# A second sorting pass in chunks of 12 tiles instead of 11, with a run-time check of the row count

## The chip, the cores and the metric

The kernel runs on one core of a Trainium2 chip. A core has a matrix engine (TensorE, PE), a vector engine (VectorE, DVE), an activation engine (ScalarE, ACT), a general engine (GpSimd, POOL) and a sync engine (SyncE, SP). Each takes its instructions from a queue of its own, in order, and they meet through semaphores. The metric is the device time of one execution in microseconds (us); lower is better.

## The reference

The reference is a message-passing layer on a graph with N = 10,000 nodes and E = 640,000 edges. Each node has 64 channels of 4 components. For each edge the source node's features are gathered, multiplied with a small tensor product of the edge's direction, scaled per channel, and summed into the destination node. At the end the channels are mixed.

```python
R = _silu(edge_feat @ w_rad)                        # (E, C), C = 64
xs = x[src]                                         # (E, C, M), M = 4
tp = jnp.einsum('eci,ef,ifo->eco', xs, Y, cg)       # (E, C, M)
msg = R[:, :, None] * tp
agg = _segment_sum(msg.reshape(-1, C * M), dst, N).reshape(N, C, M)
return jnp.einsum('ncm,cd->ndm', agg, w_mix)
```

`src` and `dst` are drawn at random, so the edges come in no order. An edge's own data are 9 words: one word that packs `src` and `dst`, four of `Y` and four of `edge_feat`.

## The kernel before

**The plan.** Edges are handled in tiles of 128, one edge per partition: 5000 tiles. The kernel sorts the edges by destination in two passes on the chip and then works through them bucket by bucket. The first pass sorts into 18 groups of 576 nodes each, the second sorts a group into 18 buckets of 32 nodes. The edges are taken in three parts of 1488, 1776 and 1736 tiles (`SPLIT`). Part 0's first pass runs alone at the beginning. After that three things run side by side, interleaved: the first pass of the next part, the second pass of the next group, and the messages of the current group.

**A pass** (`Pass`, `tables`, `route`) works in chunks of `T` tiles. In both passes a tile's edges are moved by a product with a one-hot matrix, so that the edges of one bucket come together in rows of `r` edges (`r` = 14 in the first pass, 15 in the second). A chunk ends as one array of 128 rows, which one indirect transfer of POOL stores to the rows' places in memory (`store`, line 615; `grp` is the memory of the first pass and `bkt` that of the second). The second pass has `carry`: a bucket's row that is not full at the end of a chunk is not stored but taken over into the next chunk by one more product (line 606). The first pass has T = 12, the second T = 11. The assertion in `Pass` keeps the number of rows of a chunk to 128 at most, in the worst case of all destinations.

**Per chunk**, `route` issues these steps: DVE builds a mask of slots (line 571) and spreads the edges' 9 words over the `r` slots (`X`, line 574). Then the one-hot matrices `oh` are made: `act` of a chunk's tiles on ACT, as a square per tile into `sq` (line 596) and one Relu over all of them (line 597), the others in one comparison on DVE (line 590). `act` is 6 in the first part's first pass and 7 afterwards. With a carried row one more square belongs to ACT. PE multiplies tile by tile into one bank of PSUM (lines 604 and 606), ACT evicts it into `rt` (line 611), and POOL stores it some chunks later. Every two chunks there are also products for the places (534, 536), an eviction (544) and a reduction on DVE (553), and every four chunks three small DVE instructions (559 to 563). `tables` runs once per group in the second pass: it counts the edges of each bucket in each chunk and turns the counts into row numbers; `inc[:N, B - 1:]` in it is the number of rows of each chunk.

**Messages** (`messages`) work in units of 5 tiles (part 0) or 6 (parts 1 and 2): 313 units of part 0, 626 each of parts 1 and 2. Per unit POOL gathers the source features tile by tile (line 911, into `xg`, seven buffers, issued five units ahead), ACT and PE make the radial factor (`pre`, lines 934 to 945), DVE multiplies (line 963) and builds the one-hot factor `S` (953, 956), and PE sums into `G` (line 976). DVE or ACT takes `G` out, from part 1 on with the sum of the part before, fetched from memory through the SP queue (`old`, line 990; `sums`, line 1009). In the last part the mixing product (line 1024) and the output follow.

**What sets the order.** For PE, DVE and ACT the order after the first stage is written out by hand: `groups` walks through the messages' steps and takes from the second pass so many steps per message step that a group is sorted when its messages are due (`pass2_steps`, which counts four steps per chunk). The first stage, with part 0's first pass, has its hand-written order for SP alone; there a planner orders the other engines. POOL's order after the first stage is the planner's too. A sorted group is loaded on the SP queue (line 818) when all its stores have landed; fetches of `old` and stores of `sums` are on the same queue.

**The end.** Rows that found no place in their bucket are kept in an overflow area. `overflow` runs once per pass at the end: it turns the count into a number of loop turns, loads that into registers, and handles 128 edges per turn (`body`).

Of the kernel before, what the change touches and what calls it, by code (L numbers as in the profile page):

```python
# [33 lines left out]
BT = 17  # L34
# [6 lines left out]
FAR = 2097152.0  # L41
# [4 lines left out]
class Pass:  # L46


    def __init__(self, T, r, cap, act, carry):
        self.T, self.r, self.cap, self.act, self.carry = T, r, cap, act, carry  # L50
        self.stride = 1 << (cap + P - 1).bit_length()
        self.rw = r * W

        assert T * P + B * (2 * r - 2 if carry else r - 1) < (P + 1) * r and cap >= P


def weave(main, side, ratio):
# [16 lines left out]
class Kernel:  # L74
    def __init__(self, ctx, tc, x, src, dst, Y, ef, w_rad, cg, w_mix, out):
# [16 lines left out]
        N, E, T, r = self.N, self.E, 12, 14  # L92
# [13 lines left out]
                            for m in e])  # L106
        NG = self.NG
        self.p1 = Pass(T, r, max(map(max, self.gt)) * P // r, 6, False)
        self.p2 = Pass(11, 15, BT * P // 15, 6, True)

        self.gbase = [[(k * NG + g) * self.p1.stride + self.p1.cap - self.gt[k][g] * P // r for g in range(NG)]
                      for k in range(len(SPLIT))]
# [10 lines left out]
            q.rows = q.none  # L123
        self.p1.key, self.p2.key = "grp", "bkt"
        self.xw = max(q.T * q.rw for q in (self.p1, self.p2))
        assert max(q.T + q.carry for q in (self.p1, self.p2)) <= 12

        self.p1.NC, self.p2.NC = 24, max(-(-t // self.p2.T) for t in sum(self.gt, []))
        self.p1.dst = self.dr.tile([self.p1.rows, self.p1.rw], F, name="grp")
# [14 lines left out]
    def consts(self):  # L144
        nc, c = self.nc, self.cst
# [24 lines left out]
        d = iota("dif", [[1, P]], cm=-1, at=self.ph)  # L170
# [47 lines left out]
        self.bn = iota("bn", [[NB, B]])  # L218
        self.bc = c.tile([P, B], F, name="bc")
        nc.vector.memset(self.bc, float(self.p2.cap))  # L220

    def clear_groups(self, k, eng):

# [127 lines left out]
    def tables(self, ps, D, nt, rows, kov, base, cap):  # L351
# [4 lines left out]
        nc, wk, T, r, J, H = self.nc, self.ph, ps.T, ps.r, B + 1, 64  # L356
        N = (nt + T - 1) // T
# [19 lines left out]
        n = w("n", B)  # L377
        nc.vector.tensor_copy(n[:H], sums[:, :, T])
        R = w("R", B)
# [17 lines left out]
        if ps.carry:  # L397

            f, part = w("f", B), w("part", B)
# [11 lines left out]
        inc, st = w("inc", B), w("st", J)  # L411
        nc.vector.tensor_tensor_scan(inc[:H], self.ones[:H, :B], R[:H], 0.0, op0=OP.mult, op1=OP.add)
        nc.vector.tensor_tensor(st[:H, :B], inc[:H], R[:H], op=OP.subtract)
        nc.vector.tensor_copy(st[:N, B:], inc[:N, B - 1:])

        first = w("first", B)
        at = wk.tile([P, XW], F, name="at", tag="x1" + ps.key, bufs=1)[:, :T * B]
# [40 lines left out]
        if ps.carry:  # L458
# [7 lines left out]
                                           op0=OP.is_equal, op1=OP.mult)  # L466
# [7 lines left out]
                                       op0=OP.is_le, op1=OP.mult)  # L474
# [5 lines left out]
        di = w("di", NC, d=I32)  # L480
# [33 lines left out]
    def route(self, ps, quad, nt, table):  # L514
# [5 lines left out]
        N = (nt + T - 1) // T  # L520
# [59 lines left out]
        def rows(c):  # L580

            row, _ = MS[c // (2 * Q)]
            o = c % (2 * Q) * T
            m = min(T, nt - c * T)
            (_, _, _, tg), i = table(c)
            on = ps.carry and i > 0
            oh = self.ph.tile([P, 12, P], F, name="oh", bufs=3)
            v = max(m - ps.act, 0)
            if v:
                nc.vector.tensor_tensor(oh[:, :v, :], self.v128.unsqueeze(1).to_broadcast([P, v, P]),  # L590
                                        row[:, o:o + v].unsqueeze(2).to_broadcast([P, v, P]), op=OP.is_equal)

            at = [row[:, o + u:o + u + 1] for u in range(v, m)] + ([tg[:, i - 1:i]] if on else [])
            sq = self.ph.tile([P, ps.act + 1, P], F, name="sq")
            for u, to in enumerate(at):
                nc.scalar.activation(sq[:, u, :], self.i128, AF.Square, bias=to, scale=-1.0)  # L596
            nc.scalar.activation(oh[:, v:v + len(at), :], sq[:, :len(at), :], AF.Relu, bias=self.ones[:, 0:1], scale=-2.0)  # L597
            XO[c] = (XO[c], oh, m, on)
# [538 lines left out]
    def overflow(self, ps, count):  # L1137
# [12 lines left out]
        n = nc.values_load(ni, min_val=0, max_val=(ps.rows - ps.ovf) * ps.r // P)  # L1150
        flat = ps.dst.rearrange("r w -> (r w)")

        def body(k):
            pay = wk.tile([P, W], F, name="opay")
            nc.sync.dma_start(pay, flat[bass.ds(k * (P * W) + ps.ovf * ps.rw, P * W)].rearrange("(s w) -> s w", w=W))  # L1155
            si = wk.tile([P, 1], I32, name="osi")
            nc.vector.tensor_scalar(si, pay[:, 0:1].bitcast(I32), (1 << 14) - 1, None, op0=OP.bitwise_and)  # L1157
# [5 lines left out]
            xg = wk.tile([P, 64, 4], F, name="oxg")  # L1163
            nc.gpsimd.indirect_dma_start(  # L1164
                out=xg.rearrange("p c i -> p (c i)"), out_offset=None, in_=self.x,
                in_offset=bass.IndirectOffsetOnAxis(ap=si, axis=0))

            pd = pm_.tile([P, 512], F, name="opd", tag="misc", bufs=1)
            nc.tensor.matmul(pd[:, :P], dst.to_broadcast([P, P]), self.ident, start=True, stop=True)
            eq = wk.tile([P, P], F, name="oeq")  # L1170
            nc.vector.tensor_scalar(eq, pd[:, :P], dst, None, op0=OP.is_equal)

            dup = wk.tile([P, P], F, name="odup")
            nc.vector.tensor_tensor(dup, eq, self.L, op=OP.mult)
            skip = wk.tile([P, 1], F, name="oskip")
            nc.vector.tensor_reduce(skip, dup, axis=AX.X, op=OP.max)
            em = wk.tile([P, 1], F, name="oem")
            nc.vector.tensor_scalar(em, dst, 0.5, None, op0=OP.is_lt)
            nc.vector.tensor_tensor(skip, skip, em, op=OP.max)
            di = wk.tile([P, 1], I32, name="odi")  # L1180
            nc.vector.scalar_tensor_tensor(skip, skip, FAR, dst, op0=OP.mult, op1=OP.add)
            nc.vector.tensor_scalar(di, skip, -1.0, None, op0=OP.add)
            cur = wk.tile([P, 256], F, name="ocur")
            nc.vector.memset(cur, 0.0)
            nc.gpsimd.indirect_dma_start(
                out=cur, out_offset=None, in_=self.out, in_offset=bass.IndirectOffsetOnAxis(ap=di, axis=0),
                bounds_check=self.N - 1, oob_is_err=False)

            pT = pm_.tile([P, 512], F, name="opT", tag="misc", bufs=1)
            nc.tensor.transpose(pT[:W, :P], pay, self.ident)  # L1190
            sT = wk.tile([W, P], F, name="osT")
            nc.scalar.activation(sT, pT[:W, :P], AF.Copy)
            pr = pm_.tile([P, 512], F, name="opr", tag="misc", bufs=1)
            nc.tensor.matmul(pr[:, :80], sT, self.wo, start=True, stop=True)
            R = wk.tile([P, 64], F, name="oR")
            nc.scalar.activation(R, pr[:, :64], AF.Silu)
            A = wk.tile([P, 16], F, name="oA")
            nc.scalar.activation(A, pr[:, 64:80], AF.Copy)
            V = wk.tile([P, 64, 4], F, name="oV")
            nc.vector.tensor_tensor(V, xg, R.unsqueeze(2).to_broadcast([P, 64, 4]), op=OP.mult)  # L1200
            M = wk.tile([P, 64, 4], F, name="oM")
            for o in range(4):
                nc.vector.tensor_scalar(M[:, :, o], V[:, :, 0], A[:, o:o + 1], None, op0=OP.mult)
                for i in range(1, 4):
                    nc.vector.scalar_tensor_tensor(M[:, :, o], V[:, :, i], A[:, 4 * i + o:4 * i + o + 1],
                                                   M[:, :, o], op0=OP.mult, op1=OP.add)
            pm = pm_.tile([P, 2, P], F, name="opm", tag="misc", bufs=1)
            for h in range(2):
                nc.tensor.matmul(pm[:, h, :], M[:, 32 * h:32 * h + 32, :].rearrange("p c o -> p (c o)"), eq,
                                 start=True, stop=True)  # L1210
            ms = wk.tile([P, 2, P], F, name="oms")
            nc.scalar.activation(ms, pm, AF.Copy)
            po = pm_.tile([P, 512], F, name="opo", tag="misc", bufs=1)
            for h in range(2):
                nc.tensor.matmul(po[:, :256], ms[:, h, :], self.wx[:, h].rearrange("p d o -> p (d o)"),
                                 start=(h == 0), stop=(h == 1))
            nc.vector.tensor_tensor(cur, cur, po[:, :256], op=OP.add)
            nc.gpsimd.indirect_dma_start(  # L1218
                out=self.out, out_offset=bass.IndirectOffsetOnAxis(ap=di, axis=0), in_=cur, in_offset=None,
                bounds_check=self.N - 1, oob_is_err=False)  # L1220

        with tc.For_i(0, n, 1) as k:  # L1222
            body(k)

    def run(self):
        tile_pool, nc = self.tc.tile_pool, self.nc
# [63 lines left out]
```

## Time and profile before

| | us |
|---|---|
| median of 3 runs | 8613.98 |
| lowest and highest run | 8609.68, 8615.34 |
| the profiled execution | 8636.13 |
| its span, first to last instruction | 8634.0 |
| PE busy | 6890.9 |
| DVE busy | 6821.4 |
| POOL busy | 6034.7 |
| ACT busy | 4619.2 |

The span is cut by what runs: up to about 640 us part 0's first pass and the first group's second pass; from 633.6 us, the first gather, to 8549.6 us, the last one, messages; from there the last sums and the overflow loops. The last store of the first pass starts at 5558.6 us and the last of the second at 8302.1 us. Messages of part 1 begin their gathers at about 3164 us, those of part 2 at about 5964 us.

How to read the rows that follow: a group's row has its line, engine, operation, the tile that is written and those that are read, shapes and count; then busy time and mean duration of one in ns; then the engine's idle time before these instructions and what ended it. "issue" means that the engine waited for nothing that the profile shows. A wait's row has the engine and line that waited, what ended the wait, the total in us, how often, and the longest. A row of the timeline has start, duration, engine, line and operation, and in brackets the idle time before it.

### The profile page before, as it was taken

How to read it: one execution, taken by the hardware profiler on the slowest of the kernel's cores; microseconds unless marked ns; L12 is line 12 of the kernel's file. 1: busy time of each engine (PE TensorE's matmuls, PEld its weight loads, DVE VectorE, ACT ScalarE, POOL GpSimd, SP SyncE). 2: the span in 40 equal slices, each digit the busy share in tenths (PEclk: the TensorE clock that was granted, in tenths of full speed). 3: DMA queues.
4: the chain of work that ended last, by engine and by line, in shares of the span. 5: the costliest groups of instructions: out<-in, count | busy, mean ns of one | idle time of the engine just before them, and what ended most of it. 6: DMA issues, size and time to landing. Idle time of an engine off the chain costs nothing. (4 is left out here: it accounts for less than half of the span.)

```text
span 8634.0 us, 150016 instructions
## 1 busy us (share of the span) xinstructions
PE 6890.9 (80%) x52148; PEld 6320.9 (73%) x52148; DVE 6821.4 (79%) x13093; ACT 4619.2 (54%) x13164; POOL 6034.7 (70%) x6308
## 2 busy tenths in 40 slices
PE   7977888888888778888788888876888878788875
PEld 5867777777777677777777777766777767777764
DVE  7988888888888788898888988876766767676743
ACT  6867666666666465555555655534443434343421
POOL 1226777767777767777777777777777777777775
PEclk9989999999999889999999999988988989898987
DMA  9313444344434434444444444444444444444442
GB/s 160 109 58 101 121 118 119 108 115 117 122 111 116 122 104 134 134 132 138 133 132 137 133 133 133 130 139 130 128 125 125 126 124 124 122 129 124 125 123 83
DMA packets 696294, 1056.68 MB, mean 122 GB/s; under 512 B 252018, under 2 KB 500226, under 8 KB 695536
## 3 DMA queue, kind: packets, MB, share of 16 engines
q0 software_dynamic: 286560, 746.71, 30.3%
q1 hardware_dynamic: 406384, 292.76, 12.6%
q8 instruction: 412, 6.75, 0.3%
q10 hardware_dynamic: 2592, 7.63, 0.3%
q14 instruction: 346, 2.83, 0.1%
HBM read 856.08 MB, written 207.12 MB: 123 GB/s over the span
## 5 line engine op out<-in xcount | busy, mean ns | idle before, releaser
L911 POOL DMA_INDIRECT xg<-in_x_dram,sidx x5321 | 5062.5, 951 | 1713.8 <-issue 1399.6
L604 PE MATMUL pr<-X,oh 128*128 128x126 f32 (+1 forms) x21112 | 2803.6, 291 | 490.1 <-ACT rt L611 321.7
L604 PEld LDWEIGHTS pr<-X,oh 128*128 128x128 f32 x21112 | 2664.2, 202 | 584.8 <-ACT rt L611 377.8
L976 PE MATMUL G<-S,xg 128*128 128x128 f32 x21284 | 2863.7, 296 | 139.0 <-DVE Gp L1005 98.5
L976 PEld LDWEIGHTS G<-S,xg 128*128 128x128 f32 x21284 | 2715.3, 209 | 178.3 <-DVE Gp L1005 120.0
L963 DVE TENSOR_TENSOR xg<-xg,pre 128x1536 f32<-128x1536 f32 (+1 forms) x939 | 1557.8, 1659 | 888.5 <-DMA xg<-in_x_dram,sidx 648.5
L596 ACT ACTIVATE sq<-i,rowf 128x128 f32<-128x128 f32 x6403 | 1969.4, 393 | 21.7 <-DVE rowf L561 21.2
L574 DVE TENSOR_TENSOR X<-dv,Wt 128x1512 f32<-128x1512 f32 (+4 forms) x958 | 1588.4, 1658 | 221.7 <-PE pr L604 171.1
L945 ACT ACTIVATE pre<-pre 128x384 f32<-128x384 f32 (+1 forms) x939 | 431.6, 460 | 1477.3 <-PE pre L942 1125.0
L597 ACT ACTIVATE oh<-sq,ones 128x1024 f32<-128x1024 f32 (+4 forms) x958 | 1017.6, 1062 | 27.4 <-ACT sq L596 0.3
L956 DVE TENSOR_TENSOR S<-dv,pay 128x768 f32<-128x768 f32 (+1 forms) x939 | 857.4, 913 | 60.4 <-PE G L976 15.6
L615 POOL DMA_INDIRECT grp<-rt,idx x417 | 415.3, 996 | 592.5 <-ACT rt L611 256.1
L615 POOL DMA_INDIRECT bkt<-rt,idx x541 | 542.1, 1002 | 219.8 <-issue 129.2
L590 DVE TENSOR_TENSOR oh<-dv,rowf 128x512 f32<-128x512 f32 (+2 forms) x904 | 684.0, 761 | 0.5
L929 PE MATMUL pre<-identb,e 128*108 128x128 bf16 x1878 | 275.2, 230 | 418.4 <-DVE xg L963 410.9
L929 PEld LDWEIGHTS <-e 128*108 128x108 bf16 x1878 | 218.3, 133 | 496.9 <-issue 411.0
L934 ACT ACTIVATE sT<-pre 108x256 bf16<-108x256 f32 x939 | 352.3, 375 | 429.4 <-PE pre L929 428.2
L1024 PE MATMUL po<-wf,Gs 128*128 128x256 f32 (+2 forms) x1392 | 392.7, 445 | 163.6 <-DVE Gs L1005 163.3
L1024 PEld LDWEIGHTS po<-wf,Gs 128*128 128x128 f32 (+2 forms) x1392 | 284.2, 210 | 254.8 <-DVE Gs L1005 179.4
L611 ACT ACTIVATE rt<-pr 128x135 f32<-128x135 f32 (+1 forms) x958 | 258.6, 273 | 259.5 <-DMA bkt<-rt,idx 188.4
L941 PE MATMUL pre<-wr,sT 108*128 108x192 bf16 x939 | 239.7, 255 | 182.4 <-ACT sT L934 180.6
L544 ACT ACTIVATE pc<-pp 128x432 f32<-128x432 f32 (+3 forms) x506 | 243.3, 481 | 251.0 <-DVE pos L553 149.5
(240 smaller groups left out, 5347.5 us busy)
## 6 DMA issues: line engine op xcount, KB each, us to landing
xg<-in_x_dram,sidx POOLq DMA_INDIRECT x5321
sums<-Gp SPq DMA_DIRECT2D x626, 128.0 KB
old<-sums SPq DMA_DIRECT2D x626, 128.0 KB
bkt<-z SPq DMA_DIRECT2D x24, 994.5 KB
pay<-bkt SPq DMA_DIRECT2D x34, 486.0 KB
ys<-in_Y_dram SPq DMA_DIRECT2D x104, 96.0 KB
es<-in_edge_feat_dram SPq DMA_DIRECT2D x104, 96.0 KB
out_dram<-ot SPq DMA_DIRECT2D x69, 128.0 KB
```

What stands on the lines that cost most here:

```text
L574: nc.vector.tensor_tensor(X[:, :m, :].rearrange("p t (s w) -> p t s w", w=W), msk.unsqueeze(3).to_broadcast([P, m, ps.r, W]), QD[c // Q][1 ...
L590: nc.vector.tensor_tensor(oh[:, :v, :], self.v128.unsqueeze(1).to_broadcast([P, v, P]), row[:, o:o + v].unsqueeze(2).to_broadcast([P, v, P ...
L596: nc.scalar.activation(sq[:, u, :], self.i128, AF.Square, bias=to, scale=-1.0)
L597: nc.scalar.activation(oh[:, v:v + len(at), :], sq[:, :len(at), :], AF.Relu, bias=self.ones[:, 0:1], scale=-2.0)
L604: nc.tensor.matmul(pr[:, :ps.rw], oh[:, u, :], X[:, u, :], start=(u == 0), stop=(not on and u == m - 1))
L615: st = nc.gpsimd.indirect_dma_start(out=ps.dst, out_offset=bass.IndirectOffsetOnAxis(ap=idx[:, i:i + 1], axis=0), in_=RT.pop(c), in_offset ...
L911: nc.gpsimd.indirect_dma_start(out=xg[:, t, :], out_offset=None, in_=self.x, in_offset=bass.IndirectOffsetOnAxis(ap=si[:, u:u + 1], axis=0))
L929: nc.tensor.matmul(pre[:KR, 256 + 128 * h:384 + 128 * h], e[:, 36 * t:36 * t + KR], self.identb, start=True, stop=True)
L956: nc.vector.tensor_tensor(S[:, :ut], self.eq[:, :ut].unsqueeze(3).to_broadcast([P, ut, NB, 4]), pb[:, :, 1:5].unsqueeze(2).to_broadcast([P ...
L963: nc.vector.tensor_tensor(V, V, R.unsqueeze(3).to_broadcast([P, ut, 64, 4]), op=OP.mult)
L976: nc.tensor.matmul(G[:, h].rearrange("p n f -> p (n f)"), V[:, t, 32 * h:32 * h + 32, :].rearrange("p c i -> p (c i)"), S[:, t].rearrange( ...
L1024: nc.tensor.matmul(po[:nn, :256], Gs[:, h, f].rearrange("p b n -> p (b n)")[:, :nn], self.wf[:, h, f, :], start=(h + f == 0), stop=(h + f ...
```

## The change

The second pass takes 12 tiles per chunk instead of 11. Its assertion on the worst case of rows now holds for passes without carry alone. In its place `tables` keeps the largest row count of all chunks of the second pass in `most`, one value per chunk number. A new function `whole` runs behind the two overflow loops: it tests whether any count was over 128, loads the answer into registers, and in that case clears the output and handles all edges again, 128 per turn, in a general loop over 5000 tiles. Its loop body, `add`, is the former body of the overflow loop without the loads, which both loops now have for themselves. The tile of one-hot matrices has room for 13 matrices instead of 12, for 12 tiles and the carried row, and the squares `sq` have one buffer instead of two, in all stages.

```diff
-        assert T * P + B * (2 * r - 2 if carry else r - 1) < (P + 1) * r and cap >= P
+        assert (carry or T * P + B * (r - 1) < (P + 1) * r) and cap >= P
...
-        self.p2 = Pass(11, 15, BT * P // 15, 6, True)
+        self.p2 = Pass(12, 15, BT * P // 15, 6, True)
...
-        assert max(q.T + q.carry for q in (self.p1, self.p2)) <= 12
+        self.ot = max(q.T + q.carry for q in (self.p1, self.p2))
...
+        self.most = c.tile([64, 1], F, name="most")
+        nc.vector.memset(self.most, 0.0)
...
         nc.vector.tensor_copy(st[:N, B:], inc[:N, B - 1:])
+        if ps.carry:
+            nc.vector.tensor_tensor(self.most[:N], self.most[:N], inc[:N, B - 1:], op=OP.max)
...
-            oh = self.ph.tile([P, 12, P], F, name="oh", bufs=3)
+            oh = self.ph.tile([P, self.ot, P], F, name="oh", bufs=3)
...
-            sq = self.ph.tile([P, ps.act + 1, P], F, name="sq")
+            sq = self.ph.tile([P, ps.act + 1, P], F, name="sq", bufs=1)
...
-        def body(k):
+        def load(k):
             pay = wk.tile([P, W], F, name="opay")
...
+            return pay, si, dst
 
         with tc.For_i(0, n, 1) as k:
-            body(k)
+            self.add(*load(k))
+
+    def whole(self):
+
+        nc, wk = self.nc, self.ph
+        m = wk.tile([64, 1], F, name="om")
+        nc.vector.tensor_scalar(m, self.most, P + 0.5, None, op0=OP.is_ge)
+        cp = self.ps.tile([P, 512], F, name="cw", tag="misc", bufs=1)
+        nc.tensor.matmul(cp[0:1, 0:1], self.ones[:64, 0:1], m, start=True, stop=True)
+        ni = wk.tile([1, 1], I32, name="nw")
+        nc.vector.tensor_scalar(ni, cp[0:1, 0:1], 1.0, None, op0=OP.min)
+        n = nc.values_load(ni, min_val=0, max_val=1)
+        assert self.N % 125 == 0
+        zo = wk.tile([125, 256], F, name="zo")
+        nc.vector.memset(zo, 0.0)
+
+        def load(k):
+            pay = wk.tile([P, W], F, name="opay")
+            nc.vector.memset(pay, 0.0)
...
+            return pay, si, dst
+
+        with self.tc.For_i(0, n, 1):
+            nc.sync.dma_start(self.out.rearrange("(p b) f -> p b f", p=125),
+                              zo.unsqueeze(1).to_broadcast([125, self.N // 125, 256]))
+            with self.tc.For_i(0, self.NT, 1) as k:
+                self.add(*load(k))
+
+    def add(self, pay, si, dst):
...
             self.overflow(self.p1, self.kov[:, 0:1])
             self.overflow(self.p2, self.kov[:, 1:2])
+            self.whole()
```

More of the change, by code (lines that the diff above doesn't have):

```diff
@@ L1162, in body @@
             nc.vector.tensor_scalar(dst, dk, 1.0 - TD, None, op0=OP.add)
[L1163 to L1220, printed above, removed]
-        with tc.For_i(0, n, 1) as k:
-            body(k)
+            return pay, si, dst
+        with tc.For_i(0, n, 1) as k:
+            self.add(*load(k))
[14 more added lines that the diff above has]
+            nc.vector.memset(pay, 0.0)
+            si = wk.tile([P, 1], I32, name="osi")
+            dk = wk.tile([P, 1], I32, name="odk")
+            t = bass.ds(k, 1)
+            nc.sync.dma_start(si, self.src[:, t])
+            nc.sync.dma_start(dk, self.dst[:, t])
+            nc.sync.dma_start(pay[:, 1:5], self.Y[:, t, :].rearrange("p t f -> p (t f)"))
+            nc.sync.dma_start(pay[:, 5:9], self.ef[:, t, :].rearrange("p t f -> p (t f)"))
+            dst = wk.tile([P, 1], F, name="odst")
+            nc.vector.tensor_scalar(dst, dk, 1.0, None, op0=OP.add)
+            return pay, si, dst
[4 more added lines that the diff above has]
+                self.add(*load(k))
```

56 lines of the change are left out of this document (added).

## The prediction

> **What bounds the kernel now.** I read the page's shares first, then the busy time by stretch, then who waits for whom, then the order of GpSimd's (POOL's) instructions. By the shares three engines stand close together, so the shares alone name no bound. The five stretches after the first line give, for each, its length, then busy time and instruction count of PE, PE's weight loads, DVE, ACT and POOL, then clock and DMA.
>
> ```profile
> PE 6890.9 (80%) x52148; PEld 6320.9 (73%) x52148; DVE 6821.4 (79%) x13093; ACT 4619.2 (54%) x13164; POOL 6034.7 (70%) x6308
> ...
> 0.00:640.00 640.00, 504.31 (x3753) 441.50 (x3754) 549.50 (x1317) 457.42 (x1377) 137.60 (x155) 0.91 0.50 109
> ...
> 1000.00:3000.00 2000.00, 1646.61 (x12953) 1531.17 (x12953) 1697.84 (x3306) 1278.98 (x3729) 1456.49 (x1514) 0.92 0.41 117
> ...
> 3500.00:5500.00 2000.00, 1648.71 (x12902) 1535.23 (x12902) 1748.54 (x3233) 1166.44 (x3291) 1518.28 (x1582) 0.92 0.46 133
> 5500.00:8550.00 3050.00, 2379.59 (x17090) 2160.35 (x17089) 2065.62 (x3651) 1181.30 (x3232) 2310.56 (x2423) 0.89 0.44 127
> 8550.00:8634.00 84.00, 30.48 (x111) 21.24 (x110) 24.95 (x101) 3.61 (x14) 11.53 (x13) 0.58 0.05 15
> ```
>
> POOL is busy for only 76% of the two long late stretches, yet it issued 1582 transfers in 2000 us and 2423 in 3050 us: one per 1.264 and 1.259 us, the same pace under two different loads of the other engines. The order of POOL's work, around one store to `bkt`, says why.
>
> ```profile
> 7012.34 0.95 POOL L911 DMA_INDIRECT xg<-in_x_dram,sidx  x1 [0.30 <-issue]
> 7013.59 0.95 POOL L911 DMA_INDIRECT xg<-in_x_dram,sidx  x1 [0.30 <-issue]
> 7014.84 1.01 POOL L615 DMA_INDIRECT bkt<-rt,idx  x1 [0.30 <-issue]
> 7016.15 0.96 POOL L911 DMA_INDIRECT xg<-in_x_dram,sidx  x1 [0.30 <-issue]
> ```
>
> A gather takes the queue from 7013.59 to 7014.84, 1.25 us; a store from 7014.84 to 7016.15, 1.31 us. The 0.30 us before each belongs to the pace: nothing is waited for. So POOL is full there although it shows 76%. The waits (total us, times, longest us) confirm it; in order they are POOL's from 3500 to 5500 and from 1000 to 3000, DVE's from 5500 to 8550 and two from 3500 to 5500, and one of the SP queue's over the whole span.
>
> ```profile
> POOL xg L911 <- issue: 343.4, 1127, 0.3
> POOL xg L911 <- DMA grp<-rt,idx: 11.9, 39, 0.3
> ...
> POOL xg L911 <- PE G L976: 48.0, 28, 6.0
> ...
> DVE xg L963 <- DMA xg<-in_x_dram,sidx: 604.2, 154, 6.5
> ...
> DVE Gp L1005 <- DMA sums<-Gp: 44.0, 6, 15.4
> DVE xg L963 <- DMA xg<-in_x_dram,sidx: 7.0, 2, 3.7
> ...
> SPq L818 <- DMA bkt<-rt,idx: 809.6, 45, 34.8
> ```
>
> From 5500 on DVE waits 604.2 us for gathers: POOL sets the time. From 3500 to 5500 POOL's listed waits are all 0.3 us, but DVE hardly waits for gathers (7.0 us), so either could be the slower. The counts up to 3500 and up to 5500 decide: gathers issued, and units (5 gathers for the first 313, then 6) whose product DVE has begun.
>
> ```profile
> L911 POOL DMA_INDIRECT xg<-in_x_dram,sidx x1781: 942/946/1327, 633.6 to 3498.0; - x198
> L963 DVE TENSOR_TENSOR xg<-xg,pre x345: 1468/1478/1756, 716.1 to 3496.9; 128x1280 f32<-128x1280 f32 x157, 128x1536 f32<-128x1536 f32 x16
> ...
> L911 POOL DMA_INDIRECT xg<-in_x_dram,sidx x3113: 942/946/1367, 633.6 to 5497.8; - x195
> L963 DVE TENSOR_TENSOR xg<-xg,pre x567: 1468/1489/1756, 716.1 to 5496.3; 128x1280 f32<-128x1280 f32 x105, 128x1536 f32<-128x1536 f32 x84
> ```
>
> At 3500 the lead is 1781 - (1565 + 32 x 6) = 24 gathers, at 5500 it is 3113 - (1565 + 254 x 6) = 24. Two independent rates would not agree so well over 2000 us. I read it as POOL holding the others back through its stores: the load of a sorted group on the SP queue waits for the group's last store (809.6 us in 45 waits), and the partial sums that queue behind it on SP make DVE wait (44.0 us in 6). That link is inferred. From 1000 to 3000 it is the other way round: POOL waits 48.0 us for buffers that PE frees, and DVE (85%) and PE (82%) with their mutual waits set the pace.
>
> **The change, part by part.** *Chunks.* A group of part 0, 1, 2 has 95, 113, 111 tiles, the small last group 40, 47, 46. By 11 that is 9, 11, 11 chunks (4, 5, 5), by 12 it is 8, 10, 10 (4, 4, 4): 541 chunks become 488. The 53 that go are 17 of part 0 and 18 each of parts 1 and 2. Each takes with it one store on POOL, one carry product on PE, one eviction on ACT and one each of the DVE's per-chunk instructions; the tiles stay the same.
>
> ```profile
> L615 POOL DMA_INDIRECT bkt<-rt,idx x346: 971/1005/1078, 3499.3 to 8302.1; - x173
> ...
> L590 DVE TENSOR_TENSOR oh<-dv,rowf 128x512 f32<-128x512 f32 x487 | 332.2, 682 | 0.4
> L590 DVE TENSOR_TENSOR oh<-dv,rowf 128x640 f32<-128x640 f32 x292 | 238.0, 815 | 0.0
> ...
> L574 DVE TENSOR_TENSOR X<-dv,Wt 128x1485 f32<-128x1485 f32 x487 | 830.7, 1706 | 82.4 <-PE pr L604 53.8 <-DVE dv L571 0.5 <-PE pre L942 0.5
> L574 DVE TENSOR_TENSOR X<-dv,Wt 128x945 f32<-128x945 f32 x18 | 20.6, 1144 | 14.7 <-PE pr L604 13.4
> ...
> L553 DVE TENSOR_REDUCE pos<-pc 128x22 f32<-128x396 f32 x243 | 134.8, 555 | 10.5 <-ACT pc L544 10.5
> ...
> L559 DVE TENSOR_SCALAR row<-pos 128x44 int32<-128x44 f32 x104 | 24.2, 233 | 3.6
> ...
> L596 ACT ACTIVATE sq<-i,rowf 128x128 f32<-128x128 f32 x6403 | 1969.4, 393 | 21.7 <-DVE rowf L561 21.2
> ...
> L606 PE MATMUL pr<-rt,oh 128*128 128x135 f32 x974 | 198.0, 286 | 54.6 <-ACT rt L611 54.6
> ```
>
> POOL after 3500: 346 stores are left, part 2's 192 and 154 of part 1, so groups 4 to 17 of part 1. By 12 they are 18 and 14 fewer: 32 x 1.31 = 41.9 us, all on the path if POOL stays full.
>
> DVE: with 7 of a chunk's tiles on ACT, DVE's share of the one-hots grows from 4 to 5 tiles. A group of part 1 or 2 goes from 10 x 0.682 to 9 x 0.815 = +0.52 us, one of part 0 from 8 x 0.682 to 7 x 0.815 + 0.682 = +0.93. Against it: the two L574 rows differ by 0.562 us over 540 elements, 1.04 ns each, which leaves 0.16 us fixed per instruction; a chunk less saves that in L574, L571 and L553, 0.47 us. Part 0 also drops one of three groups of slots, three instructions of the kind of L559 (0.233): 0.7. The longest count adds one small instruction per group, 0.13 to 0.17 by the rows below. Sum: +0.2 us a group in parts 1 and 2, -0.1 in part 0, some +6 us in 8000, hidden wherever POOL sets the pace and 0.1% where DVE does.
>
> ACT: squares fall from 4095 to 3745 (8 fewer in a group of part 0, 6 in parts 1 and 2): 350 x 0.393 = 138 us. PE: 53 carry products in two instructions each, 53 x 2 x 0.286 = 30 us. Neither engine is full, so this counts only through shorter waits.
>
> Before 3500 these two waits (DVE for PE, PE for ACT, both from 1000 to 3000) tell what a chunk's handing over costs.
>
> ```profile
> DVE X L574 <- PE pr L604: 87.9, 33, 8.5
> ...
> PE pr L604 <- ACT rt L611: 154.5, 78, 5.1
> ```
>
> 21 of the 53 chunks go there, of 195 of the second pass (541 - 346) and, an estimate from the code's counts, 175 of the first (part 1's 148 and the start of part 2's 145): about 6%. 6% of 87.9 to 154.5 us is 5 to 9 us in 2000, 8 to 13 us in the 2860 us from 640 to 3500. I take -8 us. Ends: -27 (21 x 1.31, POOL's whole saving passed on) and +18 (17 x 0.93 + 4 x 0.52, DVE's larger one-hots with none of its savings).
>
> *One buffer of squares, in all stages.* Squares and the Relu that reads them both run on ACT, in order, so a new square after the old Relu is what the queue does anyway.
>
> ```profile
> L597 ACT ACTIVATE oh<-sq,ones 128x1024 f32<-128x1024 f32 (+4 forms) x958 | 1017.6, 1062 | 27.4 <-ACT sq L596 0.3
> ...
> L597 ACT ACTIVATE oh<-sq,ones 128x768 f32<-128x768 f32 x124 | 115.2, 929 | 0.0
> ```
>
> The Relu, which already waits for squares just written, loses 27.4 / 958 = 0.03 us; the mirror wait would cost the same, 124 x 0.03 = 4 us at most in the first stage, off the path of DVE (86% busy there). I take 0, with ends -4 and +4.
>
> *The check behind the loops, and the fallback.* After the last overflow iteration come a comparison, a one-column product, its conversion, the load of the count into registers, and a loop with no turns. The first pass's overflow loop has no turns now; its price stands here, with the small instruction nearest to the longest count's and two turns of the second loop.
>
> ```profile
> 8571.56 0.13 DVE L1149 TENSOR_SCALAR ni<-kov 1x1 int32<-1x1 f32 x1
> 8576.26 0.21 PE L1142 MATMUL cp<-kov,ones 1*16 1x1 f32 x2 [6.89 <-issue]
> ...
> 8580.64 0.15 DVE L1157 TENSOR_SCALAR osi<-opay 128x1 int32<-128x1 int32 x1 [2.98 <-DMA opay<-bkt]
> ...
> 8599.20 0.15 DVE L1157 TENSOR_SCALAR osi<-opay 128x1 int32<-128x1 int32 x1 [1.38 <-DMA opay<-bkt]
> ...
> L414 DVE COPY st<-inc 11x1 f32<-11x1 f32 (+7 forms) x85 | 11.4, 134 | 0.0
> L413 DVE TENSOR_TENSOR st<-inc,R 64x18 f32<-64x18 f32 x85 | 14.5, 170 | 2.7
> ```
>
> From the count's conversion to the first work behind the empty loop are 4.7 us. I take +5 for the new one; ends +2 and +10 (the loop is nested). It can't gain: it stands after the last work. The overflow's own three turns stay, since with carried rows a bucket's row total does not depend on the chunk.
>
> Sum: -41.9 - 8 + 0 + 5 = -45 us. The profiled execution took 8636.13 us with a span of 8634.0; the median of the runs is 8613.98, 22 us less. I take the same difference there: 8569 us, and 8591 for a profiled one.
>
> **Rivals.** *DVE is the bound in part 1 (within 0.2%).* Then part 1's 14 stores are worth nothing, and before 3500 nothing is won: -18 x 1.31 + 5 + 3 (DVE, part 1) = -16 us, 8598. For it: DVE is 87% busy from 3500 to 5500, the fullest engine on the page. Against it: the lead of 24 gathers that does not move. The Trainium skill, Perfetto Trace Analysis, section Identifying the Most-Contended Engine, takes occupancy as the sign of the bottleneck and would choose this rival, DVE's 87% over POOL's 76%; by that rule the time is 8598. The trace speaks against it in POOL's unbroken pace, which occupancy leaves out.
>
> *The single buffer breaks the overlap in the first stage (slower).* There the order on ACT isn't written out by hand, and now a chunk's squares cannot be placed ahead of the Relu before. If each of the 124 chunks then shows its Relu of 0.929 us to DVE and PE: +115, 8684. It turns the sum to slower by over 0.2% from (45 + 17) / 124 = 0.50 us a chunk. Against it: 0.3 us of waits for squares in all, and DVE, not ACT, is full there.
>
> *More is won early (faster still).* ACT and PE, relieved, free the gather buffers sooner and POOL's 48.0 us of waits go: 8521.
>
> *The fallback runs.* If a chunk had over 128 rows, 5000 turns of 18.56 us (8580.64 to 8599.20) would follow, over 90,000 us. A full chunk has 1536 / 15 = 102.4 rows and at most 18 x 28 / 15 = 33.6 more, 136; each bucket's two ends add 14 / 15 of a row on average, 119 in all; the phases of 18 buckets spread that by one or two rows. So it should not run.
>
> **How the numbers follow.** A measurement tells 0.2%, 17 us, from no change. Forecast 0.60, with its own range from 8614 - 42 - 27 + 2 - 4 = 8543 to 8614 - 42 + 18 + 10 + 4 = 8604; DVE as the bound 0.16; single buffer 0.12; more early 0.11; fallback 0.01. So faster 0.71, same 0.16, slower 0.13. The range leaves out the slower cases and most of the largest gain: 8530 to 8622.
>
> **What would show it.** Right: 488 stores to `bkt`; from 3500 to 8550 one POOL transfer per 1.26 us as before, and a group of part 2 shorter by 1.3 us; the first gather at 633.6 as before; some 5 us more behind the last scatter. Wrong: POOL waiting after 3500 (then DVE bounds part 1), the first gather later (the squares), or ACT's waits for `bkt` stores growing at the change of part.

## The result

The changed kernel takes 8537.26 us in the median of 6 runs (8534.49 to 8543.41), the kernel before 8610.93 us in 6 runs beside it: a ratio of 0.9915 with a 95% interval of 0.9905 to 0.9925, 73.7 us less. The prediction had the sign, and the time lies in its range, near the fast end; the gain forecast was 45 us.

In the page of the changed kernel the totals moved as the counts said: DVE 12 us more, ACT 151 us less, POOL 51 us less. The line is the page's first.

```profile
PE 6849.6 (80%) x51885; PEld 6294.3 (74%) x51885; DVE 6833.0 (80%) x12901; ACT 4467.9 (52%) x12655; POOL 5984.1 (70%) x6255
```

The two spans are 8634.0 and 8537.6 us, 96.4 us apart, more than the medians. So the kernel before was profiled a second time (before_again, below); that execution had a span of 8605.1 us. Against it the spans differ by 67.5 us, 6 us less than the medians, and these can be laid out by part. The next rows are the busy time by stretch, first of the second execution of the kernel before, then of the changed kernel; each stretch begins with a part's first gather, the last ends with the last gather. The columns are the stretch, its length, then busy time and count of PE, weight loads, DVE, ACT and POOL, clock and DMA.

```profile
617.70:3136.10 2518.40, 2056.11 (x16232) 1907.81 (x16232) 2154.58 (x4271) 1621.09 (x4724) 1815.30 (x1888) 0.92 0.40 115
3136.10:5935.80 2799.70, 2251.75 (x17580) 2096.89 (x17581) 2378.25 (x4427) 1553.55 (x4370) 2114.36 (x2206) 0.91 0.46 133
5935.80:8520.40 2584.60, 2036.17 (x14488) 1844.36 (x14488) 1716.69 (x2999) 980.98 (x2683) 1958.85 (x2053) 0.89 0.43 125
```

```profile
614.00:3108.60 2494.60, 2041.02 (x16132) 1902.07 (x16133) 2152.49 (x4162) 1553.28 (x4508) 1796.88 (x1870) 0.92 0.40 116
3108.60:5885.40 2776.80, 2231.63 (x17475) 2079.01 (x17474) 2383.82 (x4384) 1511.64 (x4222) 2096.86 (x2186) 0.91 0.46 134
5885.40:8448.30 2562.90, 2045.20 (x14416) 1854.95 (x14415) 1726.99 (x2953) 936.54 (x2542) 1942.34 (x2037) 0.87 0.43 126
```

| | before, second execution | after | difference |
|---|---|---|---|
| to the first gather | 617.7 | 614.0 | -3.7 |
| part 0's gathers | 2518.4 | 2494.6 | -23.8 |
| part 1's gathers | 2799.7 | 2776.8 | -22.9 |
| part 2's gathers | 2584.6 | 2562.9 | -21.7 |
| from the last gather's start to the end | 84.7 | 89.3 | +4.6 |

How far such lengths can be trusted is shown by two kernels below that differ little from these: the same parts take 2519.3, 2803.7 and 2585.7 us in sq1_only, 2497.0, 2778.6 and 2564.5 us in no_check. So a difference of up to 4 us in a part means nothing here, and the 3.7 us before the first gather are no part of the gain: the first gather is at 609.4 us in sq1_only and at 609.8 in no_check.

In part 2 POOL issued 2053 transfers before, one per 1.259 us, and 2037 after, one per 1.258: the pace is the same and the number fell. In part 1 it is 1.269 and 1.270 us. Of the 17, 18 and 18 chunks that the parts save, the rows show 18, 20 and 16, because a part's second pass begins before its messages do, and a transfer across the border of two stretches counts in both. DVE's waits from 3500 to 5500 us in the kernel before (total, times, longest), and then POOL's and DVE's in the changed kernel:

```profile
DVE X L574 <- PE pr L604: 45.7, 21, 7.5
DVE Gp L1005 <- DMA sums<-Gp: 44.0, 6, 15.4
...
DVE Gp L1005 <- issue: 31.3, 4, 15.8
```

```profile
POOL xg L915 <- issue: 345.2, 1133, 0.3
...
DVE Gp L1009 <- DMA sums<-Gp: 67.6, 8, 24.2
DVE Gp L1009 <- issue: 60.9, 6, 15.6
...
DVE X L578 <- PE pr L608: 22.9, 15, 5.8
```

POOL's 0.3 us steps are there as before. DVE's waits for PE fell from 45.7 to 22.9 us, and its waits around the partial sums, which come over the SP queue, grew from 44.0 + 31.3 to 67.6 + 60.9. That fits a DVE that isn't the bound here: relieved in one place, it waits in another.

Of the prediction's signs of being wrong none came: POOL's listed waits from 3500 us to the last gather are of 0.3 us but for one of 5.2, the first gather is not later, and ACT's longest wait for stores to `bkt`, at the change to part 2, is 36.8 us after 42.2 in before_again.

### The profile page after: what moved, and what is told of

It is laid out like the page before. It is cut to its first block, busy times and chain, and to the rows that moved or that the text cites. A ratio compares the mean times of both kernels' runs of the same rounds, so it can differ in the third digit from the quotient of the medians.

```text
span 8537.6 us, 148817 instructions
## 1 busy us (share of the span) xinstructions
PE 6849.6 (80%) x51885; PEld 6294.3 (74%) x51885; DVE 6833.0 (80%) x12901; ACT 4467.9 (52%) x12655; POOL 5984.1 (70%) x6255
## 5 line engine op out<-in xcount | busy, mean ns | idle before, releaser
L608 PE MATMUL pr<-X,oh 128*128 128x135 f32 (+1 forms) x21112 | 2783.1, 291 | 400.2 <-ACT rt L615 256.8
L600 ACT ACTIVATE sq<-i,rowf 128x128 f32<-128x128 f32 x6106 | 1876.1, 392 | 5.6 <-DVE rowf L565 2.4
L578 DVE TENSOR_TENSOR X<-dv,Wt 128x1512 f32<-128x1512 f32 (+3 forms) x905 | 1579.7, 1746 | 147.0 <-PE pr L608 100.0
L601 ACT ACTIVATE oh<-sq,ones 128x896 f32<-128x896 f32 (+2 forms) x905 | 964.3, 1066 | 28.8 <-issue 1.4
L594 DVE TENSOR_TENSOR oh<-dv,rowf 128x640 f32<-128x640 f32 (+2 forms) x870 | 719.3, 831 | 0.5
L619 POOL DMA_INDIRECT bkt<-rt,idx x488 | 488.6, 1001 | 192.5 <-issue 111.2
L896 ACT ACTIVATE e<-er 128x360 bf16<-128x360 f32 (+3 forms) x420 | 188.9, 450 | 416.1 <-DVE er L906 415.5
L548 ACT ACTIVATE pc<-pp 128x432 f32<-128x432 f32 (+4 forms) x453 | 233.5, 515 | 254.2 <-DVE pos L557 131.9
```

What stands on the lines that cost most here:

```text
L578: nc.vector.tensor_tensor(X[:, :m, :].rearrange("p t (s w) -> p t s w", w=W), msk.unsqueeze(3).to_broadcast([P, m, ps.r, W]), QD[c // Q][1 ...
L608: nc.tensor.matmul(pr[:, :ps.rw], oh[:, u, :], X[:, u, :], start=(u == 0), stop=(not on and u == m - 1))
L619: st = nc.gpsimd.indirect_dma_start(out=ps.dst, out_offset=bass.IndirectOffsetOnAxis(ap=idx[:, i:i + 1], axis=0), in_=RT.pop(c), in_offset ...
```

## The experiments

Beside the first four experiments the kernel before took 8610 us; beside change_again, extra_squares_2, act8_2 and split_108, on another chip, 8620.6 us. Four runs (extra_squares, sq2_first, extra_products, act8) met a third chip, on which the kernel before itself takes 10,497 us; there they can be compared with each other and with the kernel before, but not with the 8537 us.

### before_again: the same kernel, a second profile

No edit.

> The kernel before, unchanged, for a second profiled execution. If the 20 us by which the first gather came earlier (633.6 us before, 614.0 after) belong to the change, the first gather stands again within some 5 us of 633.6 and the last within 15 us of 8549.6. If they belong to that one execution, the first gather comes near 614 and the span near 8611.

Measured: 8607.25 us, span 8605.1, first gather at 617.7, last at 8520.4 us. So 16 of the 20 us before the first gather, and about 12 of the 35 us in part 0, that the first two traces seemed to show belong to that one execution of the kernel before.

### sq1_only: one buffer of squares alone

```diff
-            sq = self.ph.tile([P, ps.act + 1, P], F, name="sq")
+            sq = self.ph.tile([P, ps.act + 1, P], F, name="sq", bufs=1)
```

> The kernel before with one buffer of squares and nothing else. Theory of the prediction (squares and Relu are in order on ACT anyway): 8611, within 5 us, first gather as in the kernel before. Rival (the single buffer changes the order that the planner gives the first stage, and for the better): first gather 15 to 20 us earlier, total 8591 to 8596. Second rival (it costs): up to 8726.

Measured: 8612.4 us in 10 runs, ratio 1.0003 (0.9993 to 1.0012); first gather at 609.4 us. The single buffer neither costs nor brings anything that can be measured here.

### no_check: without the longest count and the check

```diff
-        if ps.carry:
-            nc.vector.tensor_tensor(self.most[:N], self.most[:N], inc[:N, B - 1:], op=OP.max)
...
-            self.whole()
```

> The changed kernel without the longest count and without the check and the general loop behind it (the two other parts of the change stay). The check was priced at 5 us: 8537 - 5 = 8532, and from the last gather to the span's end 84 us instead of 89. If the longest count, one small DVE instruction per group, also costs where DVE is full, up to 9 us more is won: 8523.

Measured: 8536.18 us, ratio to the kernel before 0.9912 (0.9895 to 0.9929), not told apart from the changed kernel. The trace has the price. The rows are the last scatter and the check behind it in the changed kernel (span 8537.6), then the last scatter without the check (span 8538.1).

```profile
8530.33 1.03 POOL L1264 DMA_INDIRECT out_dram<-ocur,odi  x1 [8.68 <-DVE ocur L1263]
8533.72 0.19 PE L1178 MATMUL cw<-om,ones 64*1 64x1 f32 x2 [4.13 <-issue]
8533.94 0.14 DVE L1180 TENSOR_SCALAR nw<-cw 1x1 int32<-1x1 f32 x1 [3.90 <-PE cw L1178]
```

```profile
8533.86 1.03 POOL L1262 DMA_INDIRECT out_dram<-ocur,odi  x1 [8.68 <-DVE ocur L1261]
```

From the last scatter's start to the end it is 7.3 us with the check and 4.2 without: 3 us. The rest of the 4.6 us by which the end grew has another source: the overflow loop's first turn takes 22.9 us in the changed kernel (8477.00 to 8499.85), 23.0 in no_check and 18.6 in the kernel before, while the loop begins 2.7 us sooner after the last gather in the changed kernel. In extra_stores, which has the check as well, the first turn takes 18.7 us again, and in split_108 21.4, so neither the check nor the chunks of 12 alone make it; the cause is open.

### extra_stores: POOL's transfers put back, nothing else

`nowhere` holds an index out of bounds, so these 51 stores write nothing.

```diff
+            at = [idx[:, i:i + 1]] + ([self.nowhere] if ps.carry and N > 4 and c == 4 else [])
+            rt = RT.pop(c)
-            st = nc.gpsimd.indirect_dma_start(
-                out=ps.dst, out_offset=bass.IndirectOffsetOnAxis(ap=idx[:, i:i + 1], axis=0),
-                in_=RT.pop(c), in_offset=None, bounds_check=ps.none - 1, oob_is_err=False)
+            sts = [nc.gpsimd.indirect_dma_start(
+                out=ps.dst, out_offset=bass.IndirectOffsetOnAxis(ap=a, axis=0),
+                in_=rt, in_offset=None, bounds_check=ps.none - 1, oob_is_err=False) for a in at]
```

> The changed kernel with one more transfer on POOL for each of the 51 large groups, a store whose rows all lie outside the bounds, so that nothing is written; POOL's number of transfers is that of the kernel before again, and everything else stays. Theory (POOL's queue is the bound after 3500 us, each store 1.31 us): 31 of them fall after 3500, +41 us, 8578, and with POOL's share before 3500 passed on in part up to +55, 8592. Rival (DVE is the bound in part 1): +22 us from part 2 alone, 8559. If POOL is nowhere the bound: 8537. A store that writes nothing may be shorter than 1.31 us; then the sum goes by its measured pace.

Measured: 8590.06 us in 9 runs, ratio 0.9974 (0.9964 to 0.9984): 53 us of the 73.7 are gone again. The first rows are its three parts, the last ones POOL's order around one of the added stores.

```profile
611.60:3117.00 2505.40, 2045.03 (x16133) 1906.22 (x16134) 2147.84 (x4162) 1551.21 (x4508) 1814.15 (x1889) 0.92 0.40 116
3117.00:5916.00 2799.00, 2243.97 (x17469) 2092.57 (x17468) 2383.75 (x4384) 1510.85 (x4221) 2113.72 (x2204) 0.90 0.46 133
5916.00:8500.10 2584.10, 2062.74 (x14426) 1873.09 (x14426) 1727.91 (x2953) 934.86 (x2542) 1958.65 (x2053) 0.86 0.43 125
```

```profile
7007.96 1.00 POOL L625 DMA_INDIRECT bkt<-rt,idx  x1 [0.30 <-issue]
7009.27 1.00 POOL L625 DMA_INDIRECT bkt<-rt,nowi  x1 [0.30 <-issue]
7010.57 0.98 POOL L922 DMA_INDIRECT xg<-in_x_dram,sidx  x1 [0.30 <-DMA bkt<-rt,idx]
```

An added store takes 1.30 us of the queue (7009.27 to 7010.57) although it moves nothing. The added stores bring part 1 from 2776.8 to 2799.0 and part 2 from 2562.9 to 2584.1 us, 22.2 and 21.2 us: all but 0.7 and 0.5 us of what the change won there. By the rows the two stretches hold 34 transfers more (2186 and 2037 before, 2204 and 2053 now), 1.28 us each. DVE and ACT are as busy there as in the changed kernel, within 2 us, and the counts of PE's instructions agree within 10. So POOL's queue is the bound in both parts, which the rival with DVE as part 1's bound does not survive. In part 0 they bring 10.8 of 23.8 us back.

### change_again: the changed kernel on another chip

> The changed kernel, unchanged, beside the kernel before on the same chip as the next three, so that they have their base. On the chip of the first comparisons: 8537 beside 8610. If the chip is the one of extra_squares, sq2_first, extra_products and act8, on which the kernel before takes 10497 us and POOL's queue is not full: the theory that the gain is POOL's gives no gain there, 10480 to 10520; if the gain came from ACT, PE and fewer chunks handed over, it stays and grows, 10400 to 10440.

Measured: 8550.58 us beside 8620.63, ratio 0.9919 (0.9903 to 0.9936); parts of 2492.5, 2778.2 and 2563.7 us. This is the base of extra_squares_2, act8_2 and split_108.

### extra_squares_2 and act8_2: what ACT's relief was worth in part 0

The first repeats 349 squares, the second gives ACT an eighth tile of each chunk of the second pass.

```diff
+            if ps.carry and c % 4:
+                nc.scalar.activation(sq[:, 0, :], self.i128, AF.Square, bias=at[0], scale=-1.0)
```

```diff
-            self.p1.act = self.p2.act = 7
+            self.p1.act, self.p2.act = 7, 8
```

> The changed kernel with 349 squares done twice on ACT in the second pass, as in extra_squares, now beside the changed kernel. Of part 0's 23 us (2518.5 us from its first gather to part 1's in the second execution of the kernel before, 2495 after), POOL's transfers gave back 10.7 in extra_stores. If the other 12 are ACT's relief: part 0 at about 2507 us, total 8549. If they are not: part 0 within 4 us of 2495, total within 8 us of the changed kernel's. Parts 1 and 2 stay at 2777 and 2563 in both cases.

> The changed kernel with 8 instead of 7 of a chunk's tiles on ACT in the second pass, as in act8, now beside the changed kernel. DVE has some 58 us less to do, ACT some 217 more. If DVE sets part 0's pace: part 0 10 to 20 us shorter, 8517 to 8527. If the way through ACT does: part 0 10 to 40 us longer. Part 2, where POOL is full, stays at 2563 us.

Measured: 8563.32 us (8561.08 to 8565.65) and 8574.7 us (8569.0 to 8577.63), 13 and 24 us above the changed kernel's 8550.58. The rows are part 0 of the changed kernel (change_again), of extra_squares_2 and of act8_2.

```profile
619.10:3111.60 2492.50, 2037.06 (x16106) 1898.75 (x16107) 2146.78 (x4161) 1549.76 (x4503) 1795.87 (x1871) 0.92 0.41 117
```

```profile
620.90:3134.30 2513.40, 2050.45 (x16133) 1911.13 (x16134) 2149.70 (x4162) 1584.01 (x4622) 1798.75 (x1871) 0.92 0.40 116
```

```profile
622.40:3141.90 2519.50, 2065.08 (x16129) 1924.32 (x16130) 2129.80 (x4162) 1610.42 (x4657) 1795.30 (x1870) 0.91 0.40 115
```

In the traces the loss is in part 0: +20.9 and +27.0 us, while parts 1 and 2 stay within 3 us (2775.4 and 2563.3; 2779.7 and 2564.6). These are more than the medians' 13 and 24 us, since the profiled execution of change_again, with 8545.23 us, is the fastest of its four. 119 more ACT instructions with 34 us of work lengthen part 0 by 21 us by the traces, 13 by the medians, though ACT is busy for only 62% of it. In act8_2 DVE has 17 us less to do and part 0 is longer all the same: DVE at 86% does not set part 0's pace alone. The waits that grow are PE's for ACT's evictions; the rows are from part 0 of change_again, then of extra_squares_2, then of act8_2.

```profile
PE pr L608 <- ACT rt L615: 141.6, 67, 5.6
```

```profile
PE pr L610 <- ACT rt L617: 170.4, 74, 5.9
```

```profile
PE pr L608 <- ACT rt L615: 187.8, 81, 6.0
```

In the changed kernel's first trace the same wait is 157.4 us, so 16 of the 29 us by which extra_squares_2 is above change_again are within the spread. One such wait in extra_squares_2 shows the order on ACT: seven squares, the extra one (L602), the Relu, and only then the eviction that PE has waited for.

```profile
1661.27 2.15 ACT L600 ACTIVATE sq<-i,rowf 128x128 f32<-128x128 f32 x7
...
1663.62 0.39 ACT L602 ACTIVATE sq<-i,rowf 128x128 f32<-128x128 f32 x1
1664.03 1.15 ACT L603 ACTIVATE oh<-sq,ones 128x1024 f32<-128x1024 f32 x1
...
1665.62 0.28 ACT L617 ACTIVATE rt<-pr 128x135 f32<-128x135 f32 x1
...
1665.95 2.39 PE L610 MATMUL pr<-X,oh 128*128 128x135 f32 x9 [5.43 <-ACT rt L617]
```

An eviction stands in ACT's queue behind the squares of the next chunk, PE waits for the bank, and DVE waits for PE (60.1, 71.5 and 83.1 us in the same three). POOL in turn waits for what comes late: in part 0 its waits of over 0.4 us sum to 147.7 us in change_again, 169.5 in extra_squares_2 and 179.2 in act8_2, and these sums differ by what the lengths of part 0 differ by, within 5 us.

### The four runs on a chip where PE is slower

extra_squares and act8 have the edits just shown. sq2_first has two buffers of squares in the first stage and one afterwards; extra_products adds one product with zeros on PE for each large group.

```diff
-            sq = self.ph.tile([P, ps.act + 1, P], F, name="sq", bufs=1)
+            sq = self.ph.tile([P, ps.act + 1, P], F, name="sq", bufs=self.sq_bufs)
```

```diff
+            if ps.carry and N > 4 and c == 4:
+                nc.tensor.matmul(pr[:, :ps.rw], oh[:16, 0, :], self.zr[:, :ps.rw], start=False, stop=False)
```

> The changed kernel with 349 squares done twice on ACT in the second pass (in chunks 1, 2, 3, 5, 6, 7 and 9 of a group), 349 x 0.392 = 137 us of ACT, so that ACT has as many squares as in the kernel before. If part 0's gain of 35 us (first gather to part 1's first gather, 2530 us before and 2495 after) came from ACT's relief: +15 to +35 us, all before 3200 us, 8552 to 8572. If it came from POOL or from fewer chunks handed over: 8537, within 8 us. After 5500 us no change in either.

> The changed kernel with two buffers of squares in the first stage again (one afterwards, as in the changed kernel). If the single buffer made the first stage faster: first gather back at about 633 us, 8552 to 8557. If it had no part in it: first gather at 614, 8537, within 5 us.

> The changed kernel with one more product with zeros on PE for each of the 51 large groups (two PE instructions of some 0.29 us), so that PE has the carry products' time of the kernel before again, 51 x 0.58 = 30 us. If PE's relief earned part 0's gain: up to +10 us (17 groups x 0.58), 8547. Otherwise 8537, within 5 us.

> The changed kernel with 8 of a chunk's 12 tiles on ACT in the second pass, 4 on DVE as with 11 tiles. DVE has 434 fewer tiles of one-hots, some 434 x 0.133 = 58 us, ACT 434 more squares with their share of the Relu, some 434 x 0.5 = 217 us. If DVE sets the pace in part 0: some 20 us faster, 8517. If the hand-overs to and from ACT do: 10 to 40 us slower, 8547 to 8577. After 5500 us, where POOL is full, no change.

Measured: 10551.85, 10522.81, 10517.61 and 10576.07 us beside 10496.59 for the kernel before, ratios of 1.0056, 1.0025, 1.0022 (1.0012 to 1.0031) and 1.0069. The rows are one stretch of the changed kernel on the first chip, then two of extra_products and its POOL waits from 1000 to 3000 us.

```profile
1000.00:3000.00 2000.00, 1643.09 (x13032) 1533.74 (x13031) 1731.76 (x3316) 1250.46 (x3635) 1463.60 (x1523) 0.92 0.41 119
```

```profile
0.00:640.00 640.00, 507.86 (x3749) 442.48 (x3749) 546.40 (x1309) 462.35 (x1373) 137.47 (x151) 0.91 0.49 108
...
1000.00:3000.00 2000.00, 1500.04 (x10552) 1364.76 (x10552) 1405.14 (x2694) 1015.13 (x2952) 1161.66 (x1205) 0.84 0.33 94
```

```profile
POOL xg L917 <- issue: 252.8, 827, 0.7
POOL xg L917 <- PE G L982: 173.1, 62, 8.4
```

The first stage is as fast as elsewhere; then PE gets through 10,552 instructions in 2000 us where it did 13,032 in the changed kernel, at a granted clock of 0.84 instead of 0.92, and POOL waits 173.1 us for PE. Why is open. One question of the four is answered: the first gather is at 640.5 us with two buffers of squares in the first stage and at 637.2 (extra_squares), 638.1 (extra_products) and 646.9 us (act8) with one, so no part of the single buffer in the first stage is to be seen. Among themselves, extra_squares is 29 us and act8 53 us slower than sq2_first, as on the other chip in sign, and extra_products is 5 us faster, within the spread of its runs. The price of PE's products alone was not measured on a chip where POOL is full. What the runs suggest besides, and no more, is that the gain is not there when POOL's queue has room: sq2_first, the changed kernel but for the first stage's buffers, is 26 us slower than the kernel before. The changed kernel itself did not run on that chip.

### split_108: a faster version

If POOL's stores are the bound in parts 1 and 2, the next chunk to save is part 2's last one: 111 tiles are 9 chunks and 3 tiles.

```diff
-SPLIT = ((0.3, (5,)), (0.355, (6,)), (0.345, (6,)))
+SPLIT = ((0.3, (5,)), (0.365, (6,)), (0.335, (6,)))
```

> The changed kernel with four chunks of the first pass moved from part 2 to part 1 (1824 and 1688 tiles instead of 1776 and 1736). A large group of part 2 then has 108 tiles, 9 chunks instead of 10, and one of part 1 has 116, still 10. Theory (POOL is the bound in parts 1 and 2): part 2 is 17 x 1.31 = 22 us shorter, part 1 4 x 1.31 = 5 us shorter by the first pass's stores; part 0 is up to 13 us longer, as four more chunks of the first pass run beside it: 8537 - 22 - 5 + 13 = 8523. A turn less or more of the overflow loop behind it would change this by 18 us either way. If the stores of part 2 are worth nothing: 8545.

Measured: 8512.88 us (8510.61 to 8517.01), ratio to the kernel before 0.9876 (0.9859 to 0.9892), 37.7 us less than the changed kernel beside it, where 14 were expected. The rows are its three parts.

```profile
618.00:3107.60 2489.60, 2048.55 (x16181) 1909.47 (x16182) 2161.82 (x4176) 1563.31 (x4534) 1799.51 (x1872) 0.91 0.41 117
3107.60:5874.10 2766.50, 2255.43 (x17518) 2100.83 (x17517) 2377.35 (x4349) 1509.42 (x4209) 2095.03 (x2183) 0.91 0.47 135
5874.10:8418.60 2544.50, 2033.62 (x14257) 1842.90 (x14256) 1709.52 (x2920) 907.62 (x2453) 1928.63 (x2021) 0.89 0.44 127
```

Part 2 is 19.2 us shorter with 16 transfers fewer (2037 to 2021), 1.2 us each, as POOL's pace says. The rest was not foreseen: part 1 is 11.7 us shorter, more than its 3 transfers fewer (2186 to 2183) account for, and part 0 did not grow (2492.5 to 2489.6) although more of the first pass runs beside it. POOL's waits of over 0.4 us fell from 17.3 to 8.1 us in part 1 and from 147.7 to 143.4 in part 0; why is open. The spans differ by 34.5 us. It beats both kernels.

## Why the prediction was right, and where its size was off

- **POOL's queue is the bound from part 1 on: right.** The sum had 1.31 us for each store that goes. Parts 1 and 2 together lost 36 transfers by the rows (4259 to 4223) and 44.6 us, 1.24 us each. extra_stores put 34 back and the time came back with them.
- **The lead of 24 gathers that does not move: a weak sign for a right conclusion.** In the second execution of the kernel before it is 37 gathers at 3500 us and 18 at 5500, in the changed kernel 18 and 13, with POOL just as much the bound. That both were 24 was chance, and the argument from it falls; what carries the conclusion is the pace and extra_stores. The two rows are gathers issued and products begun in the changed kernel up to 5500 us: 3162 - (1565 + 264 x 6) = 13.

```profile
L915 POOL DMA_INDIRECT xg<-in_x_dram,sidx x3162: 940/946/1440, 614.0 to 5499.9; - x198
L967 DVE TENSOR_TENSOR xg<-xg,pre x577: 1468/1489/1756, 694.4 to 5499.0; 128x1280 f32<-128x1280 f32 x105, 128x1536 f32<-128x1536 f32 x88
```

- **Before 3500 us, -8 of a possible -27 to +18: the term that was mis-sized.** Part 0 alone gave 23.8 us. The step that failed scaled two waits by the share of chunks that go, 6%, and took DVE and PE for what sets the pace there. DVE's waits for PE did fall from 86.8 us in the second execution of the kernel before to 57.0, a third, but its waits for ACT's radial factor rose from 55.6 to 87.8, so they don't make the gain. What the reading missed is POOL: in part 0 its waits of over 0.4 us sum to 149.0 us before and 150.6 after, so for 94% of the part it issues at its own pace there too, and the part became shorter by what 18 transfers take. That is an account of the time and not yet a cause: when extra_stores puts the transfers back, these waits shrink to 136.3 us and only 10.8 us return. The other 13 us belong to what else goes with a chunk. ACT, counted as "not full", is the likely place, as 34 us of squares cost 13 to 21 us, but extra_squares_2 adds other work than the change took away, so how the 13 us divide is open.
- **DVE's work, +6 us: right in kind.** Its total rose by 12 us, from 6821.4 to 6833.0.
- **One buffer of squares, 0: right,** by sq1_only. The rival built on it falls.
- **The check, +5: right, 3 us by the trace.** It lies in the range of 2 to 10.
- **The offset between profile and median, 22 us, carried over: wrong.** The changed kernel's profiled execution took 8539.33 us, 2 us above its median. The 22 us were that one execution of the kernel before, in the first stage and in part 0.
- **DVE as part 1's bound, and with it the rule of occupancy:** the forecast time for that case, 8598 us, did not come, and extra_stores excludes it. The Trainium skill, Perfetto Trace Analysis, section Identifying the Most-Contended Engine, goes by occupancy and would have looked at DVE, 86% busy in part 1. The measurement speaks against it there: POOL with 76% was the bound.
- **The case of more won early** came about in part, by a third of its 48 us over the forecast -8, and not because POOL's waits for PE went: they are 51.1 us in part 0 of the changed kernel and 43.6 in the second execution of the kernel before.

## What to carry to other kernels

A queue that issues transfers can be full at a busy share of 76%: look whether its starts come at an even pace with no wait between them. Where that queue is the bound, its bound was a count here: each transfer saved was worth about one step of the pace, some 1.3 us, and a store that wrote nothing cost as much as one that wrote. An engine that is far from full, like ACT with 62%, can still cost time when short work that others wait for stands behind long work in its queue. Before a difference between two traces is explained, profile the old kernel twice: here three tenths of the difference between the first two spans belonged to one execution, and a lead of 24 gathers that looked constant was 37 and 18 in the next one.

## What the runs showed of the hardware

An indirect store whose 128 indices are all out of bounds takes 1.30 us of POOL's queue, where an ordinary store took 1.31. The first turn of the overflow loop, with the same steps in it, took 18.6 to 18.7 us in the kernel before, sq1_only and extra_stores, 22.9 to 23.0 in the changed kernel and no_check, and 21.4 in split_108. And chips differ: the kernel before took 8610, 8621 and 10,497 us on three of them, the last at a granted clock of 0.84 instead of 0.90; in extra_products there PE is slower from the second stage on.
